# Other pad sizes in SBUF: gate and value weights at 96 modulo 256 bytes, all operands of the output product at 160 modulo 256

## The chip, the cores and the metric

The kernel runs on one core of a Trainium2 chip. The metric is the device time of one execution in microseconds, lower being better. Five engines work side by side: TensorE (PE for its matmuls, PEld for its weight loads), VectorE (DVE), ScalarE (ACT), GpSimd (POOL) and SyncE (SP, which here issues DMAs). A matmul has two operands in SBUF: the stationary one (the weights, up to 128 columns, loaded into the array by a LDWEIGHTS) and the moving one, which is streamed past it column by column. The results go to PSUM.

## The reference, cut to what matters

Three layers follow each other, over 4608 tokens of 512 features:

```python
# attention with 32 pooled keys and values per head (8 batches, 8 heads, 576 tokens, 64 features)
a = softmax(phi);  k_m = a^T k;  v_m = a^T v
x = softmax(q k_m^T / 8) v_m

# experts: each token goes to the expert with the highest gate logit
h = relu(x @ w1[e]);  x = gate_w * (h @ w2[e])            # 512 -> 1024 -> 512

# gated layer
out = (sigmoid(x @ w_gate) * (x @ w_val)) @ w_out         # 512 -> 1536 -> 512
```

With these inputs all tokens go to expert 0; the code for other experts lies behind a branch that is not taken.

## The kernel before, in words

Every large product is made of three matmuls with operands in float32r: a number is split into a rounded part (name ending in h) and the rest (ending in l), and `wh·xh + wh·xl + wl·xh` is summed in PSUM (lines 400 to 402, 791 to 792, 935 to 937). So the same weights are loaded twice in a row and their lower part once.

**Stage 1, attention and expert** (to about 485 us). For each of eight batches and each half of 288 tokens, `hidden` multiplies `vmh`/`vml` (weights; w1 already folded into the pooled values by `fold_product`, lines 373 to 375) with `ahT`/`alT` (moving), 16 matmuls of 128x288 times three in all, and `y_part` multiplies `w2h`/`w2l` (weights) with `hh`/`hl` (moving): 2 x 8 x 48 = 768 matmuls of `hidden` and 1536 of `y_part`. The next batches' attention is interleaved between them as small units.

**Stage 2, gated layer** (from about 485 us). The tokens are cut into five blocks (896, 896, 896, 896 and 1024). In each block, 12 `Quad`s make the gate and value products by a scheme of seven half-size products (line 792). One quad makes seven products of six matmuls; their moving operand is half a block, 448 columns in the first four blocks and 512 in the last. That gives 4 x 504 = 2016 matmuls of 448 columns and 504 of 512. The weights are `aw` (two tiles that take turns, in the place of `w1h` and `w1l`), the moving operands are the tiles `xckv`, `xcvmh`, `xcvml`, `xcxc` (`vmh`, `vml`, `kv` and one more tile of stage 1). Then the block's output product follows (`Out.tile`): over 12 chunks of features, 7 or 8 token tiles each, three matmuls of 512 columns per tile, with `gh`/`gl` as weights (tiles in the place of `ahT`/`alT`) and `ow` as moving operand (in the place of `pht`): 12 x 36 x 3 = 1296 matmuls.

**Placement.** A pool lays its tiles out in the order in which they are first asked for, from one address upwards, each rounded up to 32 bytes; a tile with a tag takes the place of an older tile with that tag. So a small tile that nobody needs (`pad`, line 80) or that is wider than needed (`sm`, line 183: two columns are used) moves every tile behind it in its pool. All weights of a product step by 512 bytes, and the moving operands of stage 2 by 2048, so that an operand's address modulo 256 is that of its tile. Each partition has the same layout. The moving `hh` and `ahT` step by 1152 bytes, so every second operand of these lies 128 bytes further modulo 256.

The order of all work is written out in the code; nothing in it depends on addresses.

Of the kernel before, what the change touches and what calls it, by code (L numbers as in the profile page):

```python
# [9 lines left out]
F32 = mybir.dt.float32  # L10
# [8 lines left out]
P = 128  # L19
# [21 lines left out]
def attn_moe_glu_kernel(ctx: ExitStack, tc: tile.TileContext, qT, phiT, kvp, mod, wg, mbias, w1, w2, wgv, out):  # L41
    nc = tc.nc
    V, A, G, T = nc.vector, nc.scalar, nc.gpsimd, nc.tensor
# [33 lines left out]
    sp = ctx.enter_context(tc.tile_pool(name="shared", bufs=1))  # L77
    ap = ctx.enter_context(tc.tile_pool(name="apool", bufs=1))

    pad = ap.tile([P, 24], F32, name="pad")  # L80
    G.memset(pad, 0.0)
    kmb = [ap.tile([P, NP, 2 * M], F32, name=f"kmb{i}") for i in range(2)]
    vpf = ap.tile([P, NP, 2 * M], F32, name="vpf")
# [31 lines left out]
    class W1:  # L115
        def __init__(self, n, kc):
            self.w = (slice(None), slice(kc, kc + 2), slice(n * D, (n + 1) * D))
# [20 lines left out]

    w2_parts = [W2(fc) for fc in range(0, F1 // P, 2)]

    class Att:
        def __init__(self, b, pair=None):
            self.b = b
# [35 lines left out]

        def phi_softmax(self):  # L180
            pht = self.pht
            nm = ap.tile([P, 2], F32, name="nm")
            sm = ap.tile([P, 24], F32, name="sm", bufs=2)
            for g in range(2):
                V.tensor_reduce(out=nm[:, g : g + 1], in_=pht[:, g, :], axis=AX.X, op=ALU.max, negate=True)
            for g in range(2):
                one = slice(g, g + 1)
                A.activation(pht[:, g, :], pht[:, g, :], AF.Exp, bias=nm[:, one], scale=1.0, accum_out=sm[:, one])
                V.tensor_scalar_add(sm[:, one], sm[:, one], EPS)
                V.reciprocal(sm[:, one], sm[:, one])  # L190
            self.sm = sm
            self.at = ap.tile([P, NT - 1, 2 * P], F32, name="at")
# [862 lines left out]
```

## Time and profile before

| what | value |
|---|---|
| three runs | 1333.03, 1336.99, 1340.19 us (median 1336.99) |
| the profiled execution | 1338.05 us, span 1336.2 us |
| mean granted TensorE clock | 0.99 |
| PE busy | 1289.5 us, 97% of the span |
| PEld busy | 1144.4 us, 86% |
| DVE, ACT, POOL busy | 865.2, 580.0, 99.0 us |
| mean DMA rate | 130 GB/s |

The page's times of a matmul run from its start to a modelled end, and the next one starts long before that end. What a matmul costs in a steady stream is therefore the step from one start to the next. In the timeline, equal instructions that follow each other stand in one row with the start of the first; the step is the difference of two such starts over the number of matmuls between them.

### The profile page before, as it was taken

How to read it: one execution, taken by the hardware profiler on the slowest of the kernel's cores; microseconds unless marked ns; L12 is line 12 of the kernel's file. 1: busy time of each engine (PE TensorE's matmuls, PEld its weight loads, DVE VectorE, ACT ScalarE, POOL GpSimd, SP SyncE). 2: the span in 40 equal slices, each digit the busy share in tenths (PEclk: the TensorE clock that was granted, in tenths of full speed). 3: DMA queues.
4: the chain of work that ended last, by engine and by line, in shares of the span. 5: the costliest groups of instructions: out<-in, count | busy, mean ns of one | idle time of the engine just before them, and what ended most of it. 6: DMA issues, size and time to landing. Idle time of an engine off the chain costs nothing.

```text
span 1336.2 us, 19880 instructions
## 1 busy us (share of the span) xinstructions
PE 1289.5 (97%) x7648; PEld 1144.4 (86%) x7648; DVE 865.2 (65%) x1683; ACT 580.0 (43%) x1133; POOL 99.0 (7%) x96
## 2 busy tenths in 40 slices
PE   6799999999999989999999999999999999999997
PEld 5699889999999989988899888998889988788785
DVE  4788997998867448784466835668446684465532
ACT  4532423342144135563455634556345553354322
POOL 3312131312200000000000000000000000000000
PEclk9799999999999999999999999999999999999999
DMA  8455646646502023342433324333243343333112
GB/s 317 166 177 171 232 153 228 203 150 229 171 35 65 32 89 127 125 149 72 142 127 126 126 79 157 112 116 129 79 149 127 118 135 88 124 104 117 32 48 79
DMA packets 68487, 173.93 MB, mean 130 GB/s; under 512 B 6944, under 2 KB 15648, under 8 KB 65312
## 3 DMA queue, kind: packets, MB, share of 16 engines
q1 hardware_dynamic: 67376, 171.47, 38.2%
q8 instruction: 62, 1.02, 0.3%
q10 hardware_dynamic: 1008, 1.11, 0.2%
q14 instruction: 41, 0.34, 0.1%
HBM read 137.95 MB, written 34.60 MB: 129 GB/s over the span
## 4 chain that ended last, share of the span: by engine, by line
PE 58%; DMA 3%; DVE 2%; ACT 0%; issue 0%; DVEq 0%; ACTq 0%; SPq 0%
PE pstr L792 21%; PE pskv L792 10%; PE pssc L792 5%; PE psmm L937 4%; PE psmm L935 4%; PE psmm L936 4%; DMA out_dram<-ot 2%; PE pstr L935 1%; PE pstr L937 1%; PE pstr L936 1%; DMA xq<-x2d 1%; PE pssc L937 1%; PE pssc L935 1%; PE pskv L936 1%; PE pskv L937 1%; PE pssc L936 1%
## 5 line engine op out<-in xcount | busy, mean ns | idle before, releaser
L792 PE MATMUL pstr<-xcvml,aw 128*128 128x448 f32 (+1 forms) x720 | 163.2, 374 | 2.6 <-DVE gw2h L804 2.6
L400 PE MATMUL psmm<-hh,w2h 128*128 128x288 f32 x512 | 155.6, 304 | 0.0
L792 PEld LDWEIGHTS pstr<-xcvml,aw 128*128 128x128 f32 x720 | 133.6, 188 | 22.7 <-DVE gw2h L804 5.9
L401 PE MATMUL psmm<-hl,w2h 128*128 128x288 f32 x512 | 152.1, 297 | 0.0
L402 PE MATMUL psmm<-hh,w2l 128*128 128x288 f32 x512 | 151.2, 295 | 0.0
L113 DVE TENSOR_TENSOR aw<-raww,aw 128x512 fp32r<-128x512 f32 x120 | 65.9, 555 | 57.9 <-ACT aw L112 57.4
L400 PEld LDWEIGHTS psmm<-hh,w2h 128*128 128x128 f32 x512 | 96.5, 188 | 2.0
L401 PEld LDWEIGHTS psmm<-hl,w2h 128*128 128x128 f32 x512 | 96.6, 189 | 1.0
L402 PEld LDWEIGHTS psmm<-hh,w2l 128*128 128x128 f32 x512 | 96.7, 189 | 0.0
L935 PE MATMUL psmm<-ow,gh 128*128 128x512 f32 x240 | 94.8, 395 | 0.0
L936 PE MATMUL psmm<-ow,gh 128*128 128x512 f32 x240 | 94.8, 395 | 0.0
L937 PE MATMUL psmm<-ow,gl 128*128 128x512 f32 x240 | 94.8, 395 | 0.0
L418 ACT ACTIVATE hh<-psmm 128x288 fp32r<-128x288 f32 x128 | 52.0, 410 | 97.7 <-PE psmm L402 97.1
L792 PE MATMUL pstr<-xckv,aw 128*128 128x448 f32 (+1 forms) x360 | 86.7, 374 | 3.4 <-PEq L899 2.2
L792 PE MATMUL pssc<-xckv,aw 128*128 128x448 f32 (+1 forms) x360 | 86.0, 374 | 0.6 <-DVE ot L941 0.6
L792 PE MATMUL pstr<-xcvmh,aw 128*128 128x448 f32 (+1 forms) x360 | 85.5, 373 | 0.4 <-DVE tex L804 0.2
L792 PE MATMUL pskv<-xcvmh,aw 128*128 128x448 f32 (+1 forms) x360 | 85.2, 371 | 0.0
L792 PE MATMUL pskv<-xcxc,aw 128*128 128x448 f32 (+1 forms) x360 | 85.0, 371 | 0.0
L400 PE MATMUL psmm<-ahT,vmh 128*128 128x288 f32 x256 | 79.8, 312 | 3.0 <-DVE hl L419 1.0
L792 PEld LDWEIGHTS pstr<-xckv,aw 128*128 128x128 f32 x360 | 68.0, 189 | 11.7 <-issue 2.4
L113 DVE TENSOR_TENSOR aw<-sums,aw 128x512 fp32r<-128x512 f32 x120 | 77.6, 685 | 0.0
L402 PE MATMUL psmm<-ahT,vml 128*128 128x288 f32 x256 | 76.2, 298 | 1.3 <-DVE vml L389 1.3
(264 smaller groups left out, 2719.7 us busy)
## 6 DMA issues: line engine op xcount, KB each, us to landing
raww<-wd SPq DMA_DIRECT2D x60, 512.0 KB, 4.2
sums<-sd SPq DMA_DIRECT2D x48, 512.0 KB, 3.4
raw<-in_wgv_dram SPq DMA_DIRECT2D x36, 512.0 KB, 4.1
oraw<-wd SPq DMA_DIRECT2D x60, 256.0 KB, 2.7
kv<-in_kv_dram SPq DMA_DIRECT2D x9, 1024.0 KB, 9.7
qt<-in_q_dram SPq DMA_DIRECT2D x8, 1152.0 KB, 6.2
x2d<-yt SPq DMA_DIRECT2D x64, 144.0 KB, 2.0
wd<-f SPq DMA_DIRECT2D x36, 256.0 KB, 2.1
```

What stands on the lines that cost most here:

```text
L113: lo_engine.tensor_tensor(out=lo, in0=src, in1=hi.bitcast(F32), op=ALU.subtract)
L400: T.matmul(pm, wh, xh, start=i == 0, stop=False)
L401: T.matmul(pm, wh, xl, start=False, stop=False)
L402: T.matmul(pm, wl, xh, start=False, stop=i == n - 1)
L418: A.activation(self.hh[:, fc, :], pm, AF.Relu)
L792: T.matmul(o, wk, xk, start=start and k + a == 0, stop=k == KH - 1 and a == 2, skip_group_check=not start)
L935: T.matmul(o, gh, w[:, 0], start=c == 0, stop=False)
L936: T.matmul(o, gh, w[:, 1], start=False, stop=False)
L937: T.matmul(o, gl, w[:, 0], start=False, stop=c == NC2 - 1)
```

## The change

`pad` shrinks from 96 to 32 bytes, so that everything from `kmb0` up to `w2l` moves 64 bytes down. A new pad of 64 bytes behind these tiles leaves `pht` where it was, with `hh`, `hl` and all tiles of the other pool. `nm` grows from 8 to 128 bytes and `sm` shrinks from 96 to 64 (it has two buffers), so that `at` and all tiles behind it move 32 bytes up.

```diff
@@ -77,7 +77,7 @@
-    pad = ap.tile([P, 24], F32, name="pad")
+    pad = ap.tile([P, 8], F32, name="pad")
     G.memset(pad, 0.0)
@@ -138,6 +138,10 @@
     w2_parts = [W2(fc) for fc in range(0, F1 // P, 2)]
 
+    pads = [ap.tile([P, n], F32, name=f"pad{n}") for n in (16,)]
+    for t in pads:
+        G.memset(t, 0.0)
+
     class Att:
@@ -179,8 +183,8 @@
         def phi_softmax(self):
             pht = self.pht
-            nm = ap.tile([P, 2], F32, name="nm")
-            sm = ap.tile([P, 24], F32, name="sm", bufs=2)
+            nm = ap.tile([P, 32], F32, name="nm")
+            sm = ap.tile([P, 16], F32, name="sm", bufs=2)
```

The addresses that the two programs give their tiles, modulo 256 bytes (where two stand, every second operand has the second one), and how far the weights lie above the moving operand, modulo 256:

| product | weights, before and after | moving, before and after | distance, before and after |
|---|---|---|---|
| folds, 128x512 (lines 373 to 375) | `vph`, `vpl` 0, 192 | `w1h`, `w1l` 160, 96 | 96, 96 |
| `hidden`, 128x288 (400 to 402) | `vmh`, `vml` 160, 160 | `ahT`, `alT` 128/0, 160/32 | 32/160, 0/128 |
| `y_part`, 128x288 (400 to 402) | `w2h`, `w2l` 160, 96 | `hh`, `hl` 160/32, the same | 0/128, 192/64 |
| gate and value, 128x448 and 128x512 (792) | `aw` 160, 96 | `xckv` and others 160, 160 | 0, 192 |
| output, 128x512 (935 to 937) | `gh`, `gl` 128, 160 | `ow` 160, 160 | 224, 0 |

On PE, DVE, ACT and SP every instruction stands where it stood. On POOL one row is new, ahead of the first multiplications with the modality bias (`L143`; the pieces of `pad`'s own memset keep their place):

```order
 L90 MEMSET lg 128x40
 L94 TENSOR_SCALAR hits<-modt 128x40 x2
+L143 MEMSET pad_127 128x16
 L97 TENSOR_TENSOR bias_118<-hits,mb 128x320
 L97 TENSOR_TENSOR bias_119<-hits,mb 128x320
 L104 TENSOR_TENSOR bias_118<-bias_118,bias_119 128x320
```

The memset of the new pad is added; nothing else is moved.

## Rows read from the trace of the kernel before

**Rows 1.** The page: busy time, share of the span and instructions of each engine

```profile
PE 1289.5 (97%) x7648; PEld 1144.4 (86%) x7648; DVE 865.2 (65%) x1683; ACT 580.0 (43%) x1133; POOL 99.0 (7%) x96
```

**Rows 2.** Busy time by stretch: stage 1, gate and value of block 1, its output

```profile
60.00:480.00 420.00, 408.56 (x3430) 389.67 (x3429) 332.83 (x800) 144.36 (x342) 76.69 (x59) 1.00 0.44 148
498.00:604.00 106.00, 105.77 (x515) 96.06 (x514) 86.58 (x165) 62.12 (x121) 0.00 (x0) 1.00 0.41 138
604.00:656.00 52.00, 52.00 (x226) 42.15 (x225) 22.78 (x32) 18.12 (x28) 0.00 (x0) 1.00 0.38 117
```

**Rows 3.** All waits of PE from 490 us to the end: us, times, longest

```profile
PE pstr L792 <- DVE gw2h L804: 2.6, 4, 1.9
PE pssc L792 <- DVE ot L941: 0.6, 1, 0.6
PE pstr L792 <- DVE tex L804: 0.2, 1, 0.2
```

**Rows 4.** Timeline of PE, an output product: start, us, line, out<-moving,weights

```profile
1099.85 0.40 PE L935 MATMUL psmm<-ow,gh 128*128 128x512 f32 x1
1100.08 0.39 PE L936 MATMUL psmm<-ow,gh 128*128 128x512 f32 x1
1100.32 0.40 PE L937 MATMUL psmm<-ow,gl 128*128 128x512 f32 x1
1100.55 0.39 PE L935 MATMUL psmm<-ow,gh 128*128 128x512 f32 x1
...
1104.98 0.40 PE L936 MATMUL psmm<-ow,gh 128*128 128x512 f32 x1
```

**Rows 5.** Timeline of PE, gate and value of the last block

```profile
1199.69 1.52 PE L792 MATMUL pstr<-xckv,aw 128*128 128x512 f32 x6
...
1210.58 1.52 PE L792 MATMUL pssc<-xckv,aw 128*128 128x512 f32 x6
```

**Rows 6.** Timeline of PE, gate and value of block 1

```profile
540.12 1.38 PE L792 MATMUL pstr<-xckv,aw 128*128 128x448 f32 x6
...
549.85 1.38 PE L792 MATMUL pssc<-xckv,aw 128*128 128x448 f32 x6
```

**Rows 7.** Timeline of PE, gate and value of block 4

```profile
1030.41 1.40 PE L792 MATMUL pssc<-xckv,aw 128*128 128x448 f32 x6
...
1040.33 1.40 PE L792 MATMUL pstr<-xcvmh,aw 128*128 128x448 f32 x6
```

**Rows 8.** Groups by form, from 540, 690, 880 and 1030 us: busy, mean ns

```profile
L792 PE MATMUL pssc<-xckv,aw 128*128 128x448 f32 x36 | 8.3, 365 | 0.0
...
L792 PE MATMUL pssc<-xckv,aw 128*128 128x448 f32 x42 | 9.7, 365 | 0.0
...
L792 PE MATMUL pssc<-xckv,aw 128*128 128x448 f32 x24 | 5.6, 368 | 0.0
...
L792 PE MATMUL pssc<-xckv,aw 128*128 128x448 f32 x36 | 8.4, 368 | 0.0
```

**Rows 9.** Groups by form, whole span, 512 columns: output and last block

```profile
L935 PE MATMUL psmm<-ow,gh 128*128 128x512 f32 x240 | 94.8, 395 | 0.0
...
L792 PE MATMUL pssc<-xckv,aw 128*128 128x512 f32 x72 | 18.3, 389 | 0.0
```

**Rows 10.** Line 373, a fold: ns min/median/max, first and last start

```profile
L373 PE MATMUL psmm<-w1h,vph x28: 392/400/774, 42.5 to 398.8; 128*128 128x512 f32 x28
```

**Rows 11.** Line 401, `y_part` and `hidden`: ns min/median/max

```profile
L401 PE MATMUL psmm<-hl,w2h x512: 291/295/445, 62.6 to 485.1; 128*128 128x288 f32 x171
L401 PE MATMUL psmm<-alT,vmh x256: 290/296/401, 50.4 to 472.3; 128*128 128x288 f32 x128
```

**Rows 12.** Timeline of POOL, its start

```profile
1.21 0.12 POOL L81 MEMSET pad<- 128x24 f32 x1
...
22.99 1.05 POOL L288 TENSOR_TENSOR ex<-ex,sx 128x512 f32<-128x512 f32 x1 [13.64 <-DVE sx L287]
```

## The prediction

> **What bounds the kernel now.** I read the page's first section, then the busy time by stretch, then the waits of PE. PE is busy for 97% of the span [rows 1], 105.8 of 106 us while gate and value are made and all of 52 us in an output product [rows 2]; from 490 us on it waits 3.4 us in all [rows 3]. DVE is at 44% in the output stretch and at 82% in the other. So from 485 us the time is the number of matmuls times the step from one start to the next, and a change that removes no instruction can only act through that step. That is why the timeline of starts is the view that matters. It shows four steps:
> - output product, 512 columns: 22 starts from 1099.85 to 1104.98, 233.2 ns [rows 4];
> - gate and value, 512 columns: 48 starts from 1199.69 to 1210.58, 226.9 ns [rows 5];
> - gate and value, 448 columns, block 1: 48 starts in 9.73 us, 202.7 ns [rows 6];
> - the same matmuls in block 4: 48 starts in 9.92 us, 206.7 ns [rows 7].
>
> The groups' mean durations run along with the steps, about 162 ns above each: 395 against 389 ns [rows 9], 365 in blocks 1 and 2 and 368 in blocks 3 and 4 [rows 8]. So the 512-column matmul has two prices, 6.3 ns apart, and the 448-column one has two, 4.0 ns apart. The first pair differs in where weights and moving operand lie (distance 224 against 0). The second pair does not differ in any address; it is a beat that the stream of loads and matmuls falls into and keeps. Addresses are therefore one cause of the step and not the only one.
>
> **The output product.** Its weights move from 128 to 160, where `ow` already is. This is the very relation, with the same absolute addresses modulo 256 and the same 512 columns, that gate and value have in the last block of the kernel before, and these step by 226.9 ns there. 1296 matmuls x (233.2 - 226.9) = 8.2 us less. PE waits for nothing in that stretch and DVE is at 44%, so nothing stands ready to take the time back. The bound on the other side is the present step, gain 0; a loss has no row, since distance 0 is nowhere the slower one at 512 columns. I take the whole 8.2 us, as the nearest row agrees in everything but the order of PSUM banks.
>
> **Gate and value.** Their weights move from 160 to 96, under a moving operand that stays at 160: distance 192. No product of the kernel before has that distance, so it is bounded from both sides. Rows with other distances at 512 columns: 0 gives 389 ns [rows 9], 224 gives 395 [rows 9], 96 (the folds) gives a median of 400 [rows 10]. At 448 columns the present mean is 204.7 ns, as two blocks run at either beat. Lower end: the 512-column step at its better beat, less 64 columns. The worse beats show what 64 columns take: 233.2 - 206.7 = 26.5 ns, so 226.9 - 26.5 = 200.4 ns, and 2016 x (204.7 - 200.4) = 8.7 us less. A milder gain is the faster beat in all four blocks: 2016 x 2.0 = 4.0 us less. Upper end: the slow beat in all four, 4.0 us more, and the last block's 504 matmuls at the output's present step, 504 x 6.3 = 3.2 us, together 7.2 us; at the fold's price all 2520 would cost another 5 ns, 12.6 us, together 19.8 us. I take 0, between the ends, with the blocks split between the beats as now: by distance, 192 lies between 224 and 96, which are the slow ones, but weights at 96 sit like 160 halfway between multiples of 64, and both slow rows have weights at a multiple of 64 (128 and 0). The rows do not separate these two readings.
>
> **Stage 1.** `hidden` comes to distances 0/128, which `y_part` has now, and `y_part` to 192/64, which nothing has. At 288 columns the two present sets of distances differ by 1 ns (295 and 296) [rows 11], so I put both at 0, with 2304 x 1 = 2.3 us either way as the bound; the far bound is the 6.3 ns of 512 columns over the 1536 matmuls of `y_part`, 9.7 us, which I hold unlikely as distances of 0, 128, 32 and 160 all cost the same here. The folds keep distance 96: 0. The small matmuls with 8 to 128 columns are too few to matter.
>
> **The rest.** The memset of the new pad costs POOL about what the old one did, 0.12 us [rows 12], and lies in its first microseconds; POOL idles 13.6 us before its first multiplication of the softmax [rows 12]. If that cover were gone it would cost its 0.12 us. The moved tiles also are operands of DVE and ACT; in the output stretch they are idle half the time, so a change of some per cent there is hidden.
>
> **The sum.** The profiled execution took 1338.05 us, 1.85 of it outside the span; less 8.2 gives 1329.9. It lay 1.06 us above the median of the three runs, so against that median I forecast 1336.99 - 8.2 = 1328.8 us. The three runs lie 7.2 us apart; the beats alone could do that, since 2016 x 4.0 = 8.1 us lie between all blocks fast and all slow (an estimate from [rows 6, 7]). The new median has this scatter too, some 3 us either way.
>
> **The rivals.**
> 1. *The address is not the cause of the output's 233 ns.* Output and gate and value also differ in that the output changes its PSUM bank every three matmuls and the quads every six or twelve. Then the output keeps its step: 1337 us. For it: 448 columns have two steps at the same addresses. Against it: a bank change would lengthen one start in three, and in [rows 4] the steps are 230, 240, 230 ns on the timeline's 10 ns grid, with no third that stands out. The Trainium skill ("SBUF — State Buffer", section "Who interferes with whom") gives PE two independent read ports, for moving operand and weights, and says "PE and ACT never wait on anyone"; by that rule no address could matter. The two steps of the 512-column matmul speak against it as far as they come from addresses, which no single run of before can show.
> 2. *Gate and value find a better beat at 192, on top of the output's gain.* 1328.8 - 4.0 = 1324.8 to 1328.8 - 8.7 = 1320.1 us. For it: the present relation is at an edge between two beats, so a shift by 64 bytes may well land off the edge. Nothing says on which side.
> 3. *Gate and value lose what the output gains.* The slow beat throughout and the last block at 233 ns: 1328.8 + 7.2 = 1336.0 us, no change to be measured.
> 4. *Slower.* One mechanism: at 192 the weight load meets the moving stream more often, as at 224 and 96, and gate and value, with twice as many matmuls as the output, pay for it: with the output's gain and at the fold's price 1328.8 + 19.8 = 1348.6; without the output's gain 1337.0 + 7.2 = 1344.2. With the gain in hand it decides from (8.2 + 6.7) / 2520 = 5.9 ns per matmul, without it from 2.7. For it: by distance alone 192 lies between the two slow rows.
>
> **How the numbers follow.** About 0.5%, here 6.7 us, is what a measurement of this kernel can tell from no change; the bounds are 1330.3 and 1343.7 us. Chances: the forecast (output gains, gate and value as now) 0.42; rival 2 0.20; rival 3 0.13; rival 1 0.14; rival 4 0.11. The forecast lies only 1.5 us under the bound, and with some 3 us of scatter it counts as faster in about 0.27 of its 0.42; with rival 2 and a little of the others that makes 0.48 faster. Slower is rival 4 and a little of 1: 0.12. The rest, 0.40, is within 0.5%. The range runs from the better end of rival 2, a microsecond lower for the scatter, 1319, over the forecast and rivals 1 and 3 with 2.3 us for stage 1 and 3 us of scatter, to 1342; left out are rival 4 and the outermost of rival 2, about 0.15.
>
> **What would show it.** Right: the rows of lines 935 to 937 fall from 395 to 389 ns and start 227 ns apart; line 792 at 512 columns stays at 389, at 448 columns at 365 or 368 ns; `hh` and `ahT` rows stay at 295 and 296. Rival 1 shows 395 ns again. Rival 2 shows 448-column rows at 365 ns in all four blocks or near 362. Rivals 3 and 4 show 368 or more in all four, and 395 to 400 ns in the last block. The forecast fails if the output's step depends on more than the two addresses modulo 256, or if 192 is as bad for the long stream of quads as 224 is for the output.

## The result

The changed kernel takes 1327.43 us (median of six runs, 1322.92 to 1329.32); six runs of the kernel before beside it have a median of 1338.49 us (1333.03 to 1340.19). The ratio is 0.9912, with a 95% interval of 0.9887 to 0.9936: 11 us or 0.9% faster. The forecast was 1328.8 us, in a range of 1319 to 1342. The profiled execution took 1325.52 us, 12.5 less than that of before.

The page's first section, as in [rows 1]: PE loses 14.5 us of busy time, the other engines' hardly changes.

```profile
PE 1275.0 (96%) x7648; PEld 1144.2 (86%) x7648; DVE 863.4 (65%) x1683; ACT 579.8 (44%) x1133; POOL 99.5 (8%) x97
```

Lines are four higher than before (792 is now 796, 935 is 939). The groups by form over the whole span, as in [rows 9], and the line of `y_part` and `hidden`, as in [rows 11] (ns min/median/max):

```profile
L939 PE MATMUL psmm<-ow,gh 128*128 128x512 f32 x240 | 93.4, 389 | 0.0
L796 PE MATMUL pskv<-xcxc,aw 128*128 128x448 f32 x288 | 65.3, 362 | 0.0
L796 PE MATMUL pskv<-xcxc,aw 128*128 128x512 f32 x72 | 18.6, 393 | 0.0
...
L405 PE MATMUL psmm<-hl,w2h x512: 289/294/442, 63.4 to 484.6; 128*128 128x288 f32 x171
L405 PE MATMUL psmm<-alT,vmh x256: 289/294/400, 51.2 to 471.9; 128*128 128x288 f32 x128
```

The row of the kernel before for the second of these lines:

```profile
L792 PE MATMUL pskv<-xcxc,aw 128*128 128x448 f32 x288 | 66.7, 367 | 0.0
```

The output product fell from 395 to 389 ns, as forecast. The 448 columns of gate and value, which had 365 ns in two blocks and 368 in the other two [rows 8], now have 362 in all four, and their 512 columns rose from 389 to 393. The timeline of PE in block 4, where [rows 7] show the slower beat, now gives 48 starts in 9.60 us, 200.0 ns:

```profile
1029.84 1.36 PE L796 MATMUL pssc<-xckv,aw 128*128 128x448 f32 x6
...
1039.44 1.36 PE L796 MATMUL pstr<-xcvmh,aw 128*128 128x448 f32 x6
```

Steps from all starts of the two traces (the mean of those within 8 ns of their median):

| matmuls | before, ns | after, ns | all of them, us |
|---|---|---|---|
| output, 1296 of 512 columns | 233.3 | 226.8 | -8.4 |
| gate and value, 2016 of 448 | 204.4 | 200.05 | -8.8 |
| gate and value, 504 of 512 | 227.0 | 230.6 | +1.8 |
| sum | | | -15.4 |

From the first matmul of stage 2 to the last one, the two traces differ by 12.5 us. So about 3 us of the steps' gain were given back. All waits of PE from 490 us on, as in [rows 3], show the larger part, 2.5 us more:

```profile
PE pstr L796 <- DVE gw2h L808: 2.6, 4, 1.6
PE pssc L796 <- DVE ot L945: 1.7, 3, 0.8
PE pstr L796 <- DVE tex L808: 1.6, 4, 0.7
```

They lie in two places. The waits for `tex`, 1.4 us of the 2.5, lie where a block's quads end and its output begins. The timelines of PE and DVE at the end of block 1's quads:

```profile
591.68 1.48 PE L796 MATMUL pstr<-xcvmh,aw 128*128 128x448 f32 x6 [0.67 <-DVE tex L808]
...
591.01 0.62 DVE L808 TENSOR_TENSOR tex<-pstr,tex 128x448 f32<-128x448 f32 x1
```

DVE comes to this sum behind the next block's moving operands, which it has been making without a pause since 587.0 us.

The waits for `ot` and `gw2h` lie where a block's output ends and the next block's quads begin. The timeline of PE, and of DVE with the idle time ahead of each row, at the start of block 2 of the changed kernel, then DVE's row of the same copy in the kernel before:

```profile
651.84 1.47 PE L796 MATMUL pssc<-xckv,aw 128*128 128x448 f32 x6 [0.84 <-DVE ot L945]
...
655.22 1.48 PE L796 MATMUL pstr<-xcvml,aw 128*128 128x448 f32 x6 [0.31 <-DVE gw2h L808]
...
651.09 0.69 DVE L945 COPY ot<-pssc 128x512 f32<-128x512 f32 x1 [4.64 <-DMA out_dram<-ot]
653.94 0.69 DVE L945 COPY ot<-psmm 128x512 f32<-128x512 f32 x1 [2.15 <-DMA out_dram<-ot]
...
652.85 0.69 DVE L941 COPY ot<-pssc 128x512 f32<-128x512 f32 x1 [3.17 <-DMA out_dram<-ot]
```

PE waits for its bank `pssc` until DVE has copied the finished output out of it, and DVE has waited 4.64 us for one of the two buffers `ot` to be stored; at the same place the kernel before waited 3.17 us. The first store is issued at 646.5 us, 1.4 us behind the load of 512 KB for the next weights, where it was 2.0 us behind it before, and the first three stores land after a median of 4.5 us instead of 3.0. The DMA issues from 645 to 652 us of the changed kernel and, in the third row, the stores from 648 to 654 us of the kernel before (count, KB each, median us to landing); then the row of line 945 on the idle time before its copies over the whole run, which was 57.4 us before:

```profile
out_dram<-ot SPq DMA_DIRECT2D x3, 256.0 KB, 4.5
raww<-wd SPq DMA_DIRECT2D x1, 512.0 KB, 5.3
...
out_dram<-ot SPq DMA_DIRECT2D x3, 256.0 KB, 3.0
...
  DMA out_dram<-ot: 67.6, 26
```

### The profile page after: what moved, and what is told of

Same layout as the page of the kernel before. It is cut to its first block, busy times and chain, and to the rows that moved or that the text cites. A ratio compares the mean times of both kernels' runs of the same rounds, so it can differ in the third digit from the quotient of the medians.

```text
span 1323.7 us, 19881 instructions
## 1 busy us (share of the span) xinstructions
PE 1275.0 (96%) x7648; PEld 1144.2 (86%) x7648; DVE 863.4 (65%) x1683; ACT 579.8 (44%) x1133; POOL 99.5 (8%) x97
## 4 chain that ended last, share of the span: by engine, by line
PE 55%; DMA 4%; DVE 2%; ACT 1%; issue 0%; DVEq 0%; ACTq 0%; SPq 0%
PE pstr L796 20%; PE pskv L796 10%; PE pssc L796 5%; PE psmm L941 4%; PE psmm L939 4%; PE psmm L940 4%; DMA out_dram<-ot 2%; DMA xq<-x2d 2%; PE pstr L941 1%; PE pstr L939 1%; PE pstr L940 1%; PE pssc L941 1%; PE pskv L941 1%; PE pssc L939 1%; PE pssc L940 1%; PE pskv L939 1%
## 5 line engine op out<-in xcount | busy, mean ns | idle before, releaser
L939 PE MATMUL psmm<-ow,gh 128*128 128x512 f32 x240 | 93.4, 389 | 0.0
L940 PE MATMUL psmm<-ow,gh 128*128 128x512 f32 x240 | 93.4, 389 | 0.0
```

Of the source, the lines that this page charges most:

```text
L939: T.matmul(o, gh, w[:, 0], start=c == 0, stop=False)
L940: T.matmul(o, gh, w[:, 1], start=False, stop=False)
```

## The experiments

Each experiment is the changed kernel or the one before with other sizes of pads, if nothing else is said. Steps are again means over all starts.

**One part alone: the output's weights.** The kernel before, with

```diff
-            nm = ap.tile([P, 2], F32, name="nm")
-            sm = ap.tile([P, 24], F32, name="sm", bufs=2)
+            nm = ap.tile([P, 32], F32, name="nm")
+            sm = ap.tile([P, 16], F32, name="sm", bufs=2)
```

> One part alone: nm and sm as in the change, pad as before, so that the output product's weights go from 128 to 160 and gate and value stay at distance 0. If the address relation of the two operands sets the step, the output's matmuls fall from 395 to 389 ns (1296 x 6.3 to 6.6 ns), gate and value keep 389 ns at 512 columns and their two beats (365 and 368 ns) at 448, and the time falls by 8.2 to 8.6 us against the kernel before (ratio 0.9938). If the output's gain in the changed kernel came from the other moved tiles or from the quads' new rhythm, the output's rows stay at 395 ns and the time does not change.

Measured: 1333.81 us, ratio 0.9949 (0.9926 to 0.9972). Groups by form, and the waits of PE from 490 us:

```profile
L935 PE MATMUL psmm<-ow,gh 128*128 128x512 f32 x240 | 93.4, 389 | 0.0
L792 PE MATMUL pskv<-xcxc,aw 128*128 128x448 f32 x288 | 66.5, 366 | 0.0
L792 PE MATMUL pskv<-xcxc,aw 128*128 128x512 f32 x72 | 18.3, 389 | 0.0
...
PE pstr L792 <- DVE gw2h L804: 3.4, 4, 2.5
PE pssc L792 <- DVE ot L941: 1.8, 3, 1.0
```

The output's matmuls have the 389 ns (step 226.8) by the move of their weights alone. The gain of these steps is the full 8.4 us, with 1.3 us from the 448 columns, which had more of the faster beat here (203.8 ns). From the first matmul of stage 2 to the last, the profiled execution took 6.1 us less. The wait for the copy `ot` is there again, 1.8 us, with the wait for `gw2h` 0.8 us longer: what the output gains, the block's change-over takes back in part. The wait for `tex` is 0.3 us here, as good as in the kernel before.

**The other part alone: gate and value.** The changed kernel, with

```diff
-            nm = ap.tile([P, 32], F32, name="nm")
+            nm = ap.tile([P, 24], F32, name="nm")
```

`nm` of 96 bytes and two `sm` of 64 take the 224 bytes that both took before, so all tiles behind them lie as in the kernel before; the two tiles themselves have other sizes than there.

> The other part alone: pad of 8 and the new pad of 16 as in the change, nm and sm as before, so that gate and value go to 96 (distance 192) and the output stays at 224. If the relation sets the step, 448 columns run at one beat of 200.0 ns (2016 x 4.4 = 8.9 us less), 512 columns at 230.6 ns (504 x 3.6 = 1.8 us more), the output stays at 395 ns; about 7 us less before waits at the blocks' starts, which gave back some 3 us in the changed kernel: 4 to 7 us less (ratio 0.995 to 0.997). If the 200 ns beat needs the output's new rhythm ahead of it, 448 columns show 365 and 368 ns again and the time rises by 1 to 2 us.

Measured: 1331.13 us, ratio 0.9952 (0.9924 to 0.998). Groups by form, and one of PE's waits from 490 us:

```profile
L939 PE MATMUL psmm<-ow,gh 128*128 128x512 f32 x240 | 94.8, 395 | 0.0
L796 PE MATMUL pskv<-xcxc,aw 128*128 128x448 f32 x288 | 65.4, 362 | 0.0
L796 PE MATMUL pskv<-xcxc,aw 128*128 128x512 f32 x72 | 18.4, 391 | 0.0
...
PE pstr L796 <- DVE tex L808: 1.1, 3, 0.4
```

The ratio is as expected. The beat of 200 ns does not need the output's move. The wait for `tex` is longer here too, with the output as slow as before. The two parts' ratios multiply to 0.9949 x 0.9952 = 0.990, within the interval of the whole change, so nothing speaks against their simply adding up.

**Distance or address: all tiles 32 bytes higher.** The changed kernel, with

```diff
+    shift = const.tile([P, 8], F32, name="shift")
+    G.memset(shift, 0.0)
     ident = const.tile([P, P], F32, name="ident")
```

> The changed kernel with 32 bytes more ahead of all tiles of both pools, so that all distances are as in it and every address is 32 higher (gate and value weights 128, moving operands and output weights 192). If only the distance counts, all steps are those of the changed kernel: 200.0 ns at 448 columns, 230.6 at 512, 227 in the output, and the time is within 2 us of it (ratio to before 0.991). If weights at a multiple of 64 are slow whatever the distance, the output goes back to 233 ns and gate and value to 206.7 ns or more: 8.5 + 13.5 us above the changed kernel, slower than before.

Measured: 1324.36 us, ratio 0.9907 (0.9878 to 0.9936). Groups by form:

```profile
L941 PE MATMUL psmm<-ow,gh 128*128 128x512 f32 x240 | 93.4, 389 | 0.0
L798 PE MATMUL pskv<-xcxc,aw 128*128 128x448 f32 x288 | 65.4, 362 | 0.0
L798 PE MATMUL pskv<-xcxc,aw 128*128 128x512 f32 x72 | 18.4, 391 | 0.0
```

The weights now stand at 128 and 192, the moving operands at 192, and the steps are 200.06, 229.2 and 226.8 ns. So the distance counts, as far as one shift can show it. The 229.2 ns lie 1.4 below the 230.6 of the changed kernel, but gate_alone, whose gate and value have that kernel's addresses, lies 1.3 below it too (229.4 ns). Weights at a multiple of 64 bytes are not slow as such.

**The other six distances.** `pad`, the new pad, and `nm` with these numbers of columns; everything else as in the changed kernel:

| run | `pad` | new pad | `nm` | distance of gate and value | of the output |
|---|---|---|---|---|---|
| w0_a224 | 48 | 40 | 48 | 96 | 64 |
| w32_a0 | 56 | 32 | 56 | 128 | 96 |
| w64_a32 | 64 | 24 | 64 | 160 | 128 |
| w192_a96 | 32 | 56 | 16 | 32 | 192 |
| w224_a192 | 40 | 48 | 40 | 64 | 32 |
| w128_a64 | 16 | 8 | 8 | 224 | 160 |

The first of them as a diff:

```diff
-    pad = ap.tile([P, 8], F32, name="pad")
+    pad = ap.tile([P, 48], F32, name="pad")
-    pads = [ap.tile([P, n], F32, name=f"pad{n}") for n in (16,)]
+    pads = [ap.tile([P, n], F32, name=f"pad{n}") for n in (40,)]
-            nm = ap.tile([P, 32], F32, name="nm")
+            nm = ap.tile([P, 48], F32, name="nm")
```

> A look at other distances: gate and value weights at 0 (distance 96), output weights at 224 (distance 64). Reading by distance on the ring of 256 bytes (0 and 192 fast, 224 and the folds' 96 slow): gate and value at 96 like the folds, 236 ns at 512 columns and about 209 at 448; the output at 64, between 0 and 96, 230 to 236 ns. Reading by multiples of 64 (a distance of a multiple of 64 is fast, any other slow): gate and value as slow as in the first reading, but the output at 64 fast, 227 to 230 ns.

> Gate and value weights at 32 (distance 128), output weights at 0 (distance 96). By distance on the ring: gate and value at 128, far from 0 and 192 alike, 233 ns or more at 512 columns and 206.7 or more at 448; output at 96 like the folds, 236 ns. By multiples of 64: gate and value fast, 227 to 230 and 200 to 203 ns; output slow, 233 to 236.

> Gate and value weights at 64 (distance 160), output weights at 32 (distance 128). By distance on the ring: gate and value at 160, next to 192, 230 to 233 ns at 512 and 200 to 206 at 448; output at 128, 233 ns or more. By multiples of 64: gate and value slow, 233 ns or more and 206.7 or more; output fast, 227 to 230.

> Gate and value weights at 192 (distance 32), output weights at 96 (distance 192). Both readings: the output at 192 as the changed kernel's last block, 229 to 231 ns, if the order of banks plays no part. Gate and value at 32: by distance on the ring near 0 but on the side of 96, 227 to 233 ns at 512 columns and 203 to 207 at 448; by multiples of 64 slow, 233 ns or more and 206.7 or more.

> Gate and value weights at 224 (distance 64), output weights at 192 (distance 32). If the distance alone sets the step, whatever the order of PSUM banks, each product takes what the other one took at the same distance: gate and value at 64 the output's 233.3 ns at 512 columns, the output at 32 gate and value's 233.3 ns. If the order of banks has a part in it, they part by some ns. At 448 columns, where no other product stands, 203 to 206 ns, as at 32 and 96.

> Gate and value weights at 128 (distance 224), output weights at 64 (distance 160). Distance alone: gate and value the output's 233.3 ns at 512 columns, the output gate and value's 233.3 ns. At 448 columns: 200 to 203 ns if the good place of 448 columns reaches from 192 towards 0, 204 to 206 if only 192 is good.

Measured, one run each: 1340.39, 1340.78, 1344.55, 1339.02, 1338.52 and 1334.22 us. The steps by distance, with those of the kernels above, in ns. At 128 the starts spread wider than 8 ns about their median, and the means there are of those within 25 ns; elsewhere that would change no mean by more than 0.4 ns. In brackets stand the steps of single blocks where they fall into two groups:

| distance, weights above moving, modulo 256 | 448 columns, gate and value | 512 columns, gate and value | 512 columns, output |
|---|---|---|---|
| 0 | 204.4 (202.7 or 206.7) | 227.0 | 226.8 |
| 32 | 204.4 | 233.3 | 233.3 |
| 64 | 202.2 | 233.3 | 233.3 |
| 96 | 204.5 (200.0 or 206.7) | 234.2 | 234.2 |
| 128 | 204.0 | 232.4 | 232.8 |
| 160 | 205.3 | 233.3 | 233.3 |
| 192 | 200.05 | 229.2 to 230.6 | 229.0 |
| 224 | 201.8 (200.0 or 204.4) | 233.3 | 233.3 |

Two rows that stand for the agreement, groups by form of w224_a192: the output at 32 and gate and value at 64.

```profile
L939 PE MATMUL psmm<-ow,gh 128*128 128x512 f32 x240 | 94.9, 395 | 0.0
...
L796 PE MATMUL pskv<-xcxc,aw 128*128 128x512 f32 x72 | 18.7, 395 | 0.0
```

The two steps of 448 columns at distance 96, from the timelines of w0_a224 in block 2 and in block 4, each pair 42 starts apart (8.40 us, 200.0 ns; 8.68 us, 206.7 ns), and the one step at 128, from w32_a0 (8.57 us, 204.0 ns):

```profile
702.38 1.36 PE L796 MATMUL pskv<-xcxc,aw 128*128 128x448 f32 x6
...
710.78 1.36 PE L796 MATMUL pskv<-xcxc,aw 128*128 128x448 f32 x6
...
1029.73 1.40 PE L796 MATMUL pstr<-xckv,aw 128*128 128x448 f32 x6
...
1038.41 1.40 PE L796 MATMUL pstr<-xckv,aw 128*128 128x448 f32 x6
...
1030.20 1.38 PE L796 MATMUL pstr<-xckv,aw 128*128 128x448 f32 x6
...
1038.77 1.38 PE L796 MATMUL pstr<-xckv,aw 128*128 128x448 f32 x6
```

Three things follow. At 512 columns the two products agree at every distance to within 0.4 ns, but for 192. There quads of gate and value have the output's 228.9 ns too, but some, in the changed kernel and in plus256, have 233.3. One product changes its PSUM bank every three matmuls and the other every six or twelve; so the order of banks plays no part, which ends rival 1. Neither of the two readings holds: a distance of 64 is a multiple of 64 and slow, and 160, next to the good 192, is slow too. And the best distance depends on the number of columns: 0 for 512, 192 for 448.

At 448 columns the distance does not fix one step. In all traces a block keeps one step from its fourth quad to its eleventh (of twelve), but at three distances the blocks of one kernel part: at 0 as in the kernel before, at 96 (200.0 ns in block 2, 206.7 in the others) and at 224 (204.4 ns in block 1, 200.0 in the others). So 200.0 ns is not reserved to 192; what 192 has is that all 24 blocks of six traces run at it. The means at 0, 96 and 224 come from one or two traces and would move if the blocks fell otherwise. Why a block takes one step or the other, and why the distance matters at all, is not settled by these runs; what they give is a table, not a mechanism.

**The period.** The changed kernel, with gate and value weights 256 bytes higher under the same moving operands:

```diff
-    pad = ap.tile([P, 8], F32, name="pad")
+    pad = ap.tile([P, 72], F32, name="pad")
```

> The changed kernel with 256 bytes more in the first pad: the gate and value weights, and all that lies behind them in this pool, move up by 256 bytes, the moving operands of gate and value stay. All addresses modulo 256 are those of the changed kernel; the distances of gate and value modulo 512 are not. If 256 bytes is the period, 448 columns take 200.0 ns, 512 columns 229 to 231, the output 226.8. If the period is longer, gate and value leave these values by some ns, as at other distances: 203 to 206 and 233 ns.

Measured, in one run: 1322.24 us, steps of 200.06, 230.0 and 226.8 ns. The 256 bytes change no step beyond its spread in the runs above; a longer period finds no support here.

**Each length at its own best distance.** The changed kernel, with the last block's weights 64 bytes up:

```diff
-            t = ap.tile([P, 2, 2 * F1], F32R, name="aw", tag="w1", bufs=2) if old is None else old
+            if old is None:
+                up = 16 if self.b + 1 == len(BLOCKS) else 0
+                t = ap.tile([P, 4 * F1 + 64], F32R, name="aw", tag="w1", bufs=2)
+                t = t[:, up : up + 4 * F1].rearrange("p (i n) -> p i n", i=2)
+            else:
+                t = old
```

> The changed kernel with the gate and value weights of the last block alone 64 bytes higher within their tile (made 256 bytes longer), so that 448 columns keep distance 192 and 512 columns get distance 0. If distance sets the step for each length of its own, 448 columns stay at 200.0 ns, 512 columns of line 792's products fall from 230.6 to 227 ns, 504 x 3.6 = 1.8 us less than the changed kernel: some 1325.6 us, ratio to before 0.990. If the better step is given back at the waits of the last block, no difference to the changed kernel.

Measured: 1324.43 us (1321.79 to 1331.13), ratio 0.9893 (0.9854 to 0.9931). Groups by form:

```profile
L801 PE MATMUL pskv<-xcxc,aw 128*128 128x448 f32 x288 | 65.4, 362 | 0.0
L801 PE MATMUL pskv<-xcxc,aw 128*128 128x512 f32 x72 | 18.3, 389 | 0.0
```

The 512 columns are back at a step of 227.2 ns, the 448 stay at 200.08. The median lies 3 us below that of the changed kernel, but the intervals of the two ratios overlap; the step is shown, the total is not separated.

**The same, with the copies' engines exchanged.**

```diff
-            (A.copy if k % 2 else V.tensor_copy)(ot, self.po[t])
+            (V.tensor_copy if k % 2 else A.copy)(ot, self.po[t])
```

> The same, and the copies of the finished output tiles change engines: those that VectorE made are made by ScalarE and the other way round. In the changed kernel the first quads of a block wait 1.7 us in all for VectorE's copy out of the PSUM bank that the second product needs. If this wait is a matter of the engine's queue, it goes and the time falls by 1 to 2 us more, to 1324; if ScalarE is as late, the wait moves to ScalarE's copies and the time is that of the run without it.

Measured: 1329.82 us (1322.76 to 1334.66), ratio 0.9928 (0.9906 to 0.995). No gain; the median is 5.4 us above that of the run without the exchange, with intervals that overlap. The waits of PE for the copy out of `pssc`, this run's row ahead of the one of the run without the exchange:

```profile
PE pssc L801 <- ACT ot L950: 0.3, 1, 0.3
```

```profile
PE pssc L801 <- DVE ot L950: 0.3, 1, 0.3
```

Since the run without the exchange had lost this wait by itself, with the same fast output, the two say little of the queue. PE's wait for `gw2h` was longer with the exchange, 4.5 us instead of 2.9. The copies, on either engine, waited mainly for the store of an `ot` buffer (56.8 us in all here, 64.7 there), so exchanging the engines leaves the cause where it was. A third `ot` buffer would test it; it was not tried.

## Why the prediction came out as it did

The time came out within 1.4 us of the forecast, but that is in part luck: gate and value gave 7.0 us more than forecast, some 3 us of the steps' gain were given back, and the three runs from which the forecast was counted have a median 1.5 us below that of the six. Against the six, the fall is 11.1 us where 8.2 was forecast.

- *What bounds the kernel*: right. No instruction left PE, no other engine's busy time moved by more than 1.8 us, and the gain went through the step from start to start.
- *The output product*: right in cause and size. Forecast 8.2 us, measured 8.4 in the steps, and the run with this part alone shows that the address did it. The row to lean on was the same matmul at the same distance elsewhere in the kernel [rows 5].
- *Gate and value*: the step that failed. The prediction took 0 between -8.7 and +19.8 us; measured were -8.8 at 448 columns and +1.8 at 512, so 7.0 less. The lower end, worked out from the better beat of 512 columns less 64 columns (200.4 ns), was met nearly exactly (200.05), but by luck: it was worked out from the step of 512 columns at distance 0, where 448 columns take 204.4, and at 192 the 512 columns take 2 to 4 ns more. The fold's price at the upper end, 5 ns above the output's step, was 1 ns at the same distance of 96 (234.2 against 233.3). What was wrong was to weigh a distance by its neighbours on the ring. For 512 columns this gave the right sign, but 448 columns have a table of their own, and no row of before held a second distance for them. What came was rival 2, held at 0.20, at 448 columns; its ground, that the present relation lies at an edge between two beats, no run shows.
- *"Nothing stands ready to take the time back"*: wrong. About 3 us were given back, and the same reckoning gives 2.2 to 3.4 us in shift32, plus256, last160 and last160_ot. The argument used DVE's busy share of 44% in the output stretch [rows 2]. What mattered was when DVE came to single pieces of work. At the end of a block's quads that is the sum `tex`: the wait for it is 0.9 to 1.6 us in five of the six traces with gate and value at 192 (0.2 in plus256) and at most 0.4 in all others. At the change to the next block it is the copy out of a PSUM bank, which waits for a store out of one of two buffers. Over the changes to blocks 2, 3 and 4 in 13 traces (all but the one with other copy engines), PE's waits in the 14 us from the issue of the first store come to 0.15 us at most where that store lands within 3.3 us, and to 0.75 to 1.5 us where it takes 4.2 or more. That the faster output makes the stores land late, by bringing them closer behind the next weights' load, is not shown: the kernel before has landings of 3.0, 3.4 and 4.4 us at distances of 1.97, 1.94 and 1.87 us behind that load. Over these changes the first store lands after 3.9 us on average with the fast output and after 3.6 with the slow one, so what sets a landing stays open, and no run took the loads away.
- *Stage 1*: taken as 0, and near it; the medians of [rows 11] moved by 1 to 2 ns down, and from the program's first matmul to the first of stage 2 it took 0.2 us less.
- *The scatter of the runs*: the prediction let the two beats of 448 columns explain it. They can move a run: block 4 has 206.7 ns in the kernel before and 202.7 in out_alone, at the same distance, which is 2 us. But they are not needed: in every trace with gate and value at 192 all four blocks have one beat, and the six runs of the changed kernel still lie 6.4 us apart. They go with the mean granted clock of each run:

| mean granted clock | time, us |
|---|---|
| 0.982 | 1328.87, 1329.32 |
| 0.986 | 1326.90, 1327.95 |
| 0.988 | 1325.52 |
| 0.989 | 1322.92 |

In other kernels' runs this holds less closely: shift32 has 1324.86 us at 0.983 and 1328.55 at 0.987. No run varied the clock by itself.

The output's 8.4 and the missed 7.0, less the 3 given back, make up the 12.5 us by which the profiled executions differ.

## What to carry to other kernels

When PE is busy throughout, read the step between the starts of equal matmuls by product: two steps for the same number of columns in one kernel, with different addresses, are a free experiment, and moving one product into the relation of the better one can be priced to a few tenths of a nanosecond. A relation that the trace does not hold cannot be read off its neighbours: each number of columns needs its own run per distance, read block by block, since a mean over blocks with two beats hides both. Before counting such a gain in full, look at the first waits at the end of the stretch that gets faster and behind it, and at what frees the buffers there, not at the engines' busy shares.

## What the runs showed of the hardware

In this kernel's streams of weight load and float32r matmul, with a load for each matmul, the step depends on how far the weights lie above the moving operand modulo 256 bytes: 226.8 to 234.2 ns for 512 columns, 200.05 to 205.3 for 448. Moving all tiles by 32 bytes (shift32), or the weights by 256 (plus256), left the steps at 200.1 and 226.8 ns; gate and value at 512 columns had 229.2 and 230.0, where two traces at the changed kernel's own addresses had 229.4 and 230.6. The Trainium skill ("SBUF — State Buffer", section "Who interferes with whom") says that PE never waits on anyone and has two independent read ports; by that alone the two addresses could not matter, while here the step varies with their distance by up to 3%. That the two reads get in each other's way is the nearest explanation, but no run shows it. At 448 columns the stream has two steps at the same addresses at distances 0 (202.7 and 206.7 ns), 96 (200.0 and 206.7) and 224 (200.0 and 204.4), and a block keeps its own from its fourth quad to its eleventh; at 192 all 24 blocks of six traces have 200.0.
